# Raw weight buffers in turn, two tiles ahead, and a new memory layout in a fused attention and mixture-of-experts kernel

## The chip, the cores and the metric

The kernel runs on one core of a Trainium2 chip. Five engines run beside each other, each with its own queue of instructions: TensorE (PE; its weight loads are listed as PEld), VectorE (DVE), ScalarE (ACT), GpSimd (POOL) and SyncE (SP), which here only issues DMA transfers. The metric is the device time of one execution in microseconds, less is better.

## What is computed

Causal attention with a decay, for 8 batches of 8 heads, 576 positions of 64; its output, 4608 tokens of 512, goes through a mixture of 8 experts, of which each token takes the one with the highest logit:

```
scores = scale * q @ k.T + (cum[:, None] - cum[None, :])   # causal, cum = cumsum(log f)
x = softmax(scores) @ v                                    # 4608 tokens x 512
logits = x @ w_gate + modality_bias[modality_id]
e = argmax(logits); gate = softmax(logits)[e]
out = gate * (maximum(x @ w1[e], 0) @ w2[e])               # w1: 8 x 512 x 1024, w2: 8 x 1024 x 512
```

With the given inputs the experts 0 to 7 get 1053, 0, 0, 0, 90, 2200, 5 and 1260 tokens.

## The kernel before, in words

**Attention** (0 to about 365 us) runs over 32 pairs of heads. For each pair TensorE makes row maxima, the negative maxima are written to the tile `Sq` by two small shift DMAs on SP (`shift_out`, L638), the scores go to `ps`, ScalarE takes the exponential (L676, L682) and rounds it to `Ph` (L697), VectorE or GpSimd make the remainder `Pl` (L709), and TensorE multiplies with `v` into `po` or `pb` (L736 to L739). After each batch the routing chain on VectorE and GpSimd (`rm`, `rd`, `rc`, `rei`, `rtot`, ...) finds each token's expert and slot, and GpSimd scatters the rows to `xs` in device memory (`xs<-x`, L847), sorted by expert.

**The experts** work on tiles of tokens of one expert: 18 full tiles of 256 (`full(t)` for t = 0 to 17), then up to 8 half tiles of 128, of which 3 have tokens (`halves`, from about 783 us). For these inputs the full tiles belong to the experts 0, 0, 0, 5, 0, 5 (eight times, tiles 5 to 12), 7 (five times). A table in memory holds each tile's expert, its slot and a flag whether the expert differs from that of the tile before. Four tiles have their table from the counts after the next to last batch; the others get theirs in tile 2 (`other_tables`, some sixty small VectorE instructions on one row).

**Weights.** W1 and W2 of an expert have 2 MB each in float32. `load_w1` and `load_w2` fetch them by two DMAs of 1 MB each into a raw buffer; both carry the flag as a condition, and move nothing if the expert has not changed. Tile 1 has buffers of its own (`raw1b`, `raw2b`), all other tiles use `raw1` and `raw2`. The view of DMA names them `raw`. Because matmuls run in two-byte types, each weight is split into a scaled high half (float16, on ScalarE, L1303; from tile 2 on the last quarter on VectorE, L1301) and a low half (bfloat16, on VectorE, L1304): `w1h`, `w1l`, `w2h`, `w2l`, each with two buffers. The scale needs the largest magnitude: `scale` runs two passes of ScalarE over the raw weight (|w| summed up, L1255, "pass" in what follows; its output goes to the high half's buffer as scratch), adds over partitions by one small matmul on TensorE (L1257) and takes four small VectorE instructions (L1260 to L1263) to the power of two in `gs`.

**One tile.** `first` makes the hidden layer: 96 matmuls into three banks `ph` (L1379), in four groups of 24; ScalarE writes `hh` (L1393), VectorE `hl` (L1395), which free the bank. The fourth group takes the first group's bank. `second` makes the output: 48 matmuls into two banks `py` (L1428), ScalarE scales them to `y` (L1434), GpSimd writes the rows out (L1437). Tokens come as `xg`; VectorE turns them (`xt`, L1241), ScalarE and VectorE split them (`xh`, `xl`, L1356, L1357). While tile t multiplies, the passes, splits and tokens of tile t+1 are made.

**The order.** Each engine works through its instructions in order. A scheduler lists them by their dependencies and by lines such as `self.order(x, behind)` and `self.in_line(...)`, which put instructions one behind the other without a wait. SP issues its DMAs in that order too: one that waits holds up those behind it.

Of the kernel before, what the change touches and what calls it, by code (L numbers as in the profile page):

```python
# [224 lines left out]
class Attn:  # L225
    def __init__(self, ctx, tc, dram, qk, v, vt, f, ids, wg, bias, xs, writers, nb=8):
# [24 lines left out]
        self.divided, self.routed, self.weighed = [], {}, []  # L251
# [381 lines left out]
    def shift_out(self, p):  # L633

        self.own(("shift", p % 3), p)
        mT = self.get("mT", p)
        for a in range(2):
            x = self.nc.sync.dma_start(self.Sq[1 + a:P:64, p % 3, :], mT[:, a])  # L638
        self.shifted = x.ins.name
# [29 lines left out]
    def exp(self, p, g):  # L669
# [4 lines left out]
        if g == 2:  # L674

            nc.scalar.activation(ps[:, :, 0:w], ps[:, :, 0:w], AF.Exp, bias=self.lnp, scale=0.125)  # L676
            self.own(("Pt", p, g), p)
            return
# [13 lines left out]
    def half(self, p, i):  # L692
# [4 lines left out]
        x = self.nc.scalar.copy(self.Ph_t[p % 2][:, :, c], self.exps(p, i))  # L697
        self.rounded = x
# [4 lines left out]
    def rest(self, p, i):  # L703
# [5 lines left out]
        e.tensor_tensor(self.Pl_t[p % 2][:, :, c], self.exps(p, i), self.Ph_t[p % 2][:, :, c], ALU.subtract)  # L709
# [7 lines left out]
    def weighted(self, u):  # L717
# [22 lines left out]
        self.weighed = self.weighed[-1:] + [(first, x)]  # L740
# [263 lines left out]
class Moe:  # L1004
    def __init__(self, keep, tc, w1, w2, xs, writers, out):
# [7 lines left out]
        self.ring("xg", keep, 3, [P, 2 * 514], F32)  # L1013
        self.ring("xa", keep, 4, [P, T // P, 2], F32)
# [37 lines left out]
    def open(self, ctx):  # L1052
# [56 lines left out]
    def slots(self, nt, num, skip, name, rows=T):  # L1109
# [11 lines left out]
        e = t([1, 1 + num, 1], F32, "e")  # L1121
        vec.tensor_reduce(e[:, 1:], le, AX.X, ALU.add)
# [5 lines left out]
        if skip is not None:  # L1128
            vec.tensor_tensor(le, self.ie.broadcast_to(s3), e[:, 1:].broadcast_to(s3), ALU.is_equal)
# [10 lines left out]
    def table(self, e, k, cum, num, name, ok=None):  # L1140
# [4 lines left out]
        vec.tensor_copy(part(0), e[:, 1:])  # L1145
# [19 lines left out]
    def other_tables(self, n):  # L1165
# [20 lines left out]
        vec.tensor_copy(e[:, 0:1], self.last)  # L1186
        vec.tensor_reduce(eh[:, 0:1], e[:, 1:], AX.XY, ALU.max)

        vec.tensor_scalar(ok, ok, -1.0, 1.0, ALU.mult, ALU.add)
        vec.scalar_tensor_tensor(e[:, 1:], ok, eh[:, 1:2, :], e[:, 1:], ALU.mult, ALU.add)  # L1190
# [56 lines left out]
    def scale(self, name, t, raw, to, behind=None):  # L1247

        nc, vec = self.nc, self.nc.vector
        am, g, e, s = (self.next(x) for x in ("am", "gm", "ge", "gs"))  # L1250
# [497 lines left out]
```

## Time and profile before

| | |
|---|---|
| median of 3 runs | 826.67 us (826.48 to 828.06) |
| the profiled execution | 828.71 us, its span 827.0 |
| mean granted clock | 0.977 |
| busy TensorE / VectorE / ScalarE / GpSimd | 762.2 / 676.7 / 676.7 / 377.8 us |
| ScalarE idle ahead of the passes over W1 (L1255) | 17.6 us, behind loads of `raw` |

Times in the rows below are microseconds from the start of the span, unless marked ns. A row of a timeline is the start, the length, the engine, the line, the operation and its output and input by name, and in brackets the time for which the engine was idle before it, with the instruction that ended the wait. A row of waits is who waited, for whom, the total, how often and the longest. The chain is followed back from the last instruction; DMA in it is the time until a load landed. PEclk is TensorE's granted clock as a share of full speed.

### The profile page before, as it was taken

To read this page: it belongs to the slowest core of one execution; us is meant where nothing else is said; L and a number is where in the kernel's file an instruction comes from. 1 tells how busy PE (TensorE), PEld (TensorE's weight loads), DVE (VectorE), ACT (ScalarE), POOL (GpSimd) and SP (SyncE) were. 2 spreads that over 40 slices of the span, in tenths; PEclk is the share of its full clock that TensorE was granted. 3 is DMA by queue.
4 is the path that set the end of the run, shared out by engine and by line. 5 is a ranking of instruction groups with operands and counts; after the bars stand their busy time and mean duration, and the time that the engine had idled before them with its cause. 6 is when DMAs were issued, how large, how long until landed. Compare 5 with 4: busy or idle time off the path is not lost.

```text
span 827.0 us, 23639 instructions
## 1 busy us (share of the span) xinstructions
PE 762.2 (92%) x9567; PEld 563.7 (68%) x9567; DVE 676.7 (82%) x1393; ACT 676.7 (82%) x839; POOL 377.8 (46%) x374
## 2 busy tenths in 40 slices
PE   8998999989998999878788979999999989999996
PEld 4787887878887887674554556666666656666563
DVE  7887898989898989677548778888888788887777
ACT  5896989898989897688837488888888778888686
POOL 9766989898989887854240111111111010112011
PEclk9998999999999999999998999999999999999999
DMA  5533454545454433294983684212111451260931
GB/s 168 202 117 116 147 172 137 171 139 170 139 170 139 164 116 112 90 327 147 294 243 115 178 259 149 53 52 52 52 52 52 132 162 33 52 238 27 353 130 39
DMA packets 67583, 117.00 MB, mean 141 GB/s; under 512 B 10827, under 2 KB 27787, under 8 KB 67468
## 3 DMA queue, kind: packets, MB, share of 16 engines
q1 hardware_dynamic: 60746, 94.39, 36.1%
q0 software_dynamic: 6704, 21.02, 7.4%
q8 instruction: 77, 1.26, 0.7%
q14 instruction: 38, 0.31, 0.1%
q10 hardware_dynamic: 18, 0.01, 0.0%
HBM read 147.98 MB, written 22.55 MB: 206 GB/s over the span
## 4 chain that ended last, share of the span: by engine, by line
PE 50%; DVE 25%; ACT 7%; DMA 7%; issue 5%; POOL 5%; SPq 0%; DVEq 0%; ACTq 0%; POOLq 0%
PE py L1428 16%; PE ph L1379 15%; PE ps L592 7%; DMA raw<-in_w_dram 6%; DVE mt L613 4%; DVE vl L560 3%; PE po L736 2%; PE po L739 2%; POOL Pl L709 2%; PE po L738 2%; DVE w1l L1304 2%; PE pb L534 2%; DVE x L751 2%; POOL L L435 2%; PE ph L1495 1%
## 5 line engine op out<-in xcount | busy, mean ns | idle before, releaser
L1437 POOL DMA_INDIRECT out_dram<-y,xa x32 | 45.1, 1410 | 308.3 <-ACT y L1434 248.7
L709 POOL TENSOR_TENSOR Pl<-Pt,Ph 128x1024 f16<-128x1024 f32 (+1 forms) x63 | 141.7, 2255 | 14.6 <-ACT Ph L697 13.6
L1379 PEld LDWEIGHTS <-w1h 128*128 128x128 f16 x1152 | 112.4, 99 | 34.3 <-ACT w1h L1303 10.2
L1428 PEld LDWEIGHTS <-hh 128*128 128x128 f16 x576 | 55.5, 99 | 82.6 <-ACT hh L1393 14.4
L736 PE MATMUL po<-vh,Ph 128*128 128x73 f16 x930 | 101.8, 200 | 3.6 <-DVE lgh L754 3.4
L592 PE MATMUL ps<-X 64*128 64x288 f32 (+5 forms) x768 | 103.4, 339 | 0.0
L739 PE MATMUL po<-vh,Pl 128*128 128x73 f16 x930 | 101.4, 199 | 0.9 <-DVE Pl L709 0.9
L738 PE MATMUL po<-vl,Ph 128*128 128x72 f16 x930 | 101.6, 197 | 0.0
L682 ACT ACTIVATE Pt<-ps,lnp 128x576 f32<-128x576 f32 (+1 forms) x96 | 81.5, 864 | 20.2 <-PE ps L592 20.1
L736 PEld LDWEIGHTS <-Ph 128*128 128x128 f16 x960 | 94.3, 99 | 4.8 <-DVE lgh L754 1.6
L738 PEld LDWEIGHTS <-Ph 128*128 128x128 f16 x960 | 95.3, 99 | 3.3 <-issue 3.1
L739 PEld LDWEIGHTS <-Pl 128*128 128x128 f16 x960 | 94.3, 98 | 1.1 <-DVE Pl L709 1.0
L435 POOL TENSOR_TENSOR L<-raw,X 128x1152 bf16<-128x1152 f32 x32 | 84.6, 2642 | 20.5 <-ACT X L429 16.3
L1379 PE MATMUL ph<-xh,w1h 128*128 128x256 f16 x576 | 82.1, 276 | 12.1 <-DVE hl L1395 6.5
L1379 PE MATMUL ph<-xl,w1h 128*128 128x256 bf16 x576 | 89.3, 275 | 0.0
L1304 DVE SCALAR_TENSOR_TENSOR w2l<-raw,gs,w2h 128x1024 bf16<-128x1024 f32 x68 | 84.0, 1281 | 4.5 <-ACT w2h L1303 3.9
L613 DVE TENSOR_REDUCE mt<-ps 128x2 f32<-128x128 f32 (+3 forms) x128 | 81.5, 682 | 6.9 <-PE ps L592 6.8
L1379 PE MATMUL ph<-xh,w1l 128*128 128x256 f16 x576 | 86.2, 274 | 0.0
L1428 PE MATMUL py<-w2h,hh 128*128 128x512 f16 x288 | 77.3, 384 | 9.2 <-ACT hh L1393 7.3
L1304 DVE SCALAR_TENSOR_TENSOR w1l<-raw,gs,w1h 128x1024 bf16<-128x1024 f32 x68 | 84.3, 1280 | 1.0 <-ACT w1h L1303 0.4
L1428 PE MATMUL py<-w2l,hh 128*128 128x512 bf16 x288 | 78.8, 389 | 1.8 <-DVE w2l L1304 1.6
L1255 ACT ACTIVATE w1h<-raw 128x2048 f16<-128x2048 f32 x34 | 64.7, 1903 | 17.6 <-DMA raw<-in_w_dram 17.6
(340 smaller groups left out, 1912.0 us busy)
## 6 DMA issues: line engine op xcount, KB each, us to landing
raw<-in_w_dram SPq DMA_DIRECT2D x80, 1024.0 KB
raw<-in_qk_dram SPq DMA_DIRECT2D x32, 608.0 KB
vT<-in_vt_dram SPq DMA_DIRECT2D x32, 320.0 KB
xg<-xs SPq DMA_DIRECT2D x64, 128.0 KB
vr<-in_v_dram SPq DMA_DIRECT2D x30, 256.0 KB
raw1b<-in_w_dram SPq DMA_DIRECT2D x6, 1024.0 KB
raw2b<-in_w_dram SPq DMA_DIRECT2D x6, 1024.0 KB
hxg<-xs SPq DMA_DIRECT2D x5, 257.0 KB
```

Source lines behind the costliest of these rows:

```text
L435: e.tensor_tensor(self.two(self.L3[p % 3]), self.two(self.get("raw", p)), self.two(f32(X)), ALU.subtract)
L592: self.nc.tensor.matmul(ps[0:m, h, c:c + w], a(r), b(r), start=start, stop=not any(x[0] is ps for x in parts[n + 1:]), skip_group_check=True)
L613: nc.vector.tensor_reduce(mt[:, :, ic:ic + 1], pm[:, :, c0:c0 + w], AX.X, ALU.max)
L682: nc.scalar.activation(self.get("Pt", (p, i))[:, :, o:o + w], ps[:, :, 0:w], AF.Exp, bias=self.lnp, scale=0.125)
L709: e.tensor_tensor(self.Pl_t[p % 2][:, :, c], self.exps(p, i), self.Ph_t[p % 2][:, :, c], ALU.subtract)
L736: x = nc.tensor.matmul(o, Ph[:, c0:c0 + P], vh[:, c, hh, :], start=(c == 0), stop=False)
L738: nc.tensor.matmul(o[:, 1:73], Ph[:, c0:c0 + P], vl[:, c, hh, :], start=False, stop=False)
L739: x = nc.tensor.matmul(o, Pl[:, c0:c0 + P], vh[:, c, hh, :], start=False, stop=(c == ic))
L1255: made.append(nc.scalar.activation(to[a], raw[a], AF.Abs, accum_out=am[:, q:q + 1]))
L1304: return x, nc.vector.scalar_tensor_tensor(low, raw, s, high, ALU.mult, ALU.subtract)
L1379: y = nc.tensor.matmul(ph[g][:, i, :], w[:, k, f0:f0 + P], x[:, k, :], start=(j == 0 and (t > 0 or i == 0)), stop=(j == len(m) - 1 and (t ...
L1428: x = nc.tensor.matmul(py, h[:, k, c * P:c * P + P], w[:, k, :], start=(j == 0), stop=(j == len(m) - 1))
```

## The change

Each of W1 and W2 gets two raw buffers for all tiles, used in turn by t % 2. Tile t's loads fetch the weights of tile t+2, and the flag compares a tile's expert with that of two tiles before (`e` has two leading entries instead of one). Full tiles' loads then move data for the tiles 0, 1, 3, 6, 13 and 14; before, for 0 to 5 and 13. The first raw buffer of W1, `raw1a`, is taken from a pool that does not share memory with attention; its two DMAs and the first pass over it are placed inside attention's last pairs. The experts' memory is laid out in another order, the raw buffers low. The rules for the order of `hh` and the splits of W2 in tile 1 are gone, and in tile 0 the order of the passes is written out anew. Nothing is removed from the arithmetic.

```diff
@@ run
-        self.load_w1(self.row[0], 0, loads)
-        self.load_w2()
-        made, m, sc = self.scale("w1", 0, self.raw1[0], self.w1h[:, 0], self.routed["w0"].ins.name)
+        made = self.load_w1(self.row[0], 0)
+        self.in_line("so", *made, "sn")
+        for x in self.load_w2(0):
+            self.order(x, self.routed["sm"].ins.name)
+        self.load_w1(self.row[1], 1)
+        self.load_w2(1)
+        made, m, sc = self.scale("w1", 0)
...
-        self.in_line("Ph", *made, *[y[0] for y in x], a[0], *[y[0] for y in more[:2]], "odds", more[2][0])
+        self.in_line("h", made[0], "e")
+        self.in_line("Ph", made[1], *[y[0] for y in x], a[0], *[y[0] for y in more])
...
@@ full(t)
-            if t == 0:
-                self.load_w1(self.row[1], 1, always=True)
-                self.load_w2(1)
-                self.load_w1(self.row[2], always=True)
-            elif t > 1:
-                self.load_w1(self.row[t + 1])
+            if t + 2 > FULL:
+                self.load_w1(self.rowh[1], 1)
+            elif t and t != TABLES:
+                self.load_w1(self.row[t + 2], t % 2)
+            ec.setdefault(t, self.ec)
...
-                if t != 1:
-                    self.load_w2()
-                return made, names
+                if t != TABLES:
+                    self.load_w2(t % 2, ec[t])
+                return names
...
+                if t == 0:
+                    a, b = self.sums2
+                    self.in_line(more[-1][0], a, "odds", b, made[0], *self.later, made[1])
@@ first(t, again)
-            if g == 0:
-                rounded, behind = again(self.summed)
+            if t and g == int(t == OTHERS):
+                behind = again(self.summed)
...
-            if t == OTHERS:
-                self.order(x, behind[min(g + 1, 3)][0])
...
@@ open: the experts' memory
+        self.raw1a = keep.tile([P, 4, 1024], F32, name="raw1a")
-        raw1 = one([P, 4, 1024], F32, "raw1")
         self.w1h = one([P, 2, 4, 1024], F16, "w1h")
+        raw2 = one([P, 8, 512], F32, "raw2")
+        self.raw1 = self.raw1a, one([P, 4, 1024], F32, "raw1b")
+        self.raw2 = raw2, one([P, 8, 512], F32, "raw2b")
...
```

("h" and "e" are the round and the exponential of pair 30, "so" and "sn" the last shift DMA of pair 30 and the first of pair 31, "odds" ScalarE's `rex` of the routing.)

Three places show what that does to the order. SP at the end of attention, before (`raw_9435` is W1's buffer, `raw_9450` W2's):

```order
L638 DMA Sq<-mT 2x5x128 x4
L1199 TENSOR_LOAD c_taba x2
L1272 ISA
L1272 DMA raw_9435<-in_w_dram 128x4x512
L1272 ISA
L1272 DMA raw_9435<-in_w_dram 128x4x512
L1286 ISA
L1286 DMA raw_9450<-in_w_dram 128x4x512
```

and now (`raw1a` is W1's first buffer, `raw_9440` W2's):

```order
L638 DMA Sq<-mT 2x5x128 x2
L1196 TENSOR_LOAD c_taba x2
L1271 ISA
L1271 DMA raw1a<-in_w_dram 128x4x512
L1271 ISA
L1271 DMA raw1a<-in_w_dram 128x4x512
L638 DMA Sq<-mT 2x5x128 x2
L1284 ISA
L1284 DMA raw_9440<-in_w_dram 128x4x512
```

The load of the first W1 has moved ahead of the last two of the four shift DMAs; its table entries are read there too.

ScalarE around tile 0's hidden layer, before (`am` takes the sum of a pass, `gs` is a scale; `raw_9450` is W2, the second `xh` tile 1's tokens):

```order
L832 ACTIVATE rex<-rd,isw 128x40
L1303 ACTIVATE w1h<-raw_9435,gs_84 128x4x256
L1255 ACTIVATE w2h,am_69<-raw_9450 128x2048 x2
L1393 ACTIVATE hh<-ph_9417 128x512
L1393 ACTIVATE hh<-ph_9418 128x512
L1303 ACTIVATE w2h<-raw_9450,gs_85 128x1024 x4
L1393 ACTIVATE hh<-ph_9416 128x512
L1356 CAST xh_9458<-px_9412 128x4x128
L1356 CAST xh_9458<-px_9431 128x4x128
```

and now (`raw_9440` is W2 of tile 0, `raw1b` W1 of tile 1):

```order
L1302 ACTIVATE w1h<-raw1a,gs_85 128x4x256 x4
L1254 ACTIVATE w2h,am_70<-raw_9440 128x2048
L831 ACTIVATE rex<-rd,isw 128x40
L1254 ACTIVATE w2h,am_70<-raw_9440 128x2048
L1254 ACTIVATE w1h,am_71<-raw1b 128x4x512
L1302 ACTIVATE w2h<-raw_9440,gs_86 128x1024 x4
L1254 ACTIVATE w1h,am_71<-raw1b 128x4x512
L1355 CAST xh_9453<-px_9413 128x4x128
L1355 CAST xh_9453<-px_9432 128x4x128
L1393 ACTIVATE hh<-ph_9418 128x512
L1393 ACTIVATE hh<-ph_9419 128x512
```

The first two `hh` stood ahead of the splits of W2; they now stand behind them, behind both passes over tile 1's W1 and behind the two `xh`.

ScalarE between the last `hh` of tile 3 and the splits of W1 for tile 4, before (`raw_9435` is W1, `py_9426` and `py_9427` the two halves of tile 3's output, `xt` the turned tokens):

```order
L1393 ACTIVATE hh<-ph_9417 128x512
L1356 CAST xh_9457<-xt_9471 128x512
L1255 ACTIVATE w1h,am_68<-raw_9435 128x4x512
L1356 CAST xh_9457<-xt_9471 128x512
L1255 ACTIVATE w1h,am_68<-raw_9435 128x4x512
L1434 ACTIVATE y_9461<-py_9426,xs_91 128x512
L1434 ACTIVATE y_9462<-py_9427,xs_91 128x512
L1303 ACTIVATE w1h<-raw_9435,gs_86 128x4x256 x3
L1255 ACTIVATE w2h,am_69<-raw_9450 128x2048 x2
```

and now (`raw1a` and `raw_9440` hold W1 and W2 of tile 4):

```order
L1393 ACTIVATE hh<-ph_9418 128x512
L1254 ACTIVATE w1h,am_69<-raw1a 128x4x512 x2
L1254 ACTIVATE w2h,am_70<-raw_9440 128x2048
L1427 ACTIVATE y_9479<-py_9427,xs_92 128x512
L1427 ACTIVATE y_9480<-py_9428,xs_92 128x512
L1254 ACTIVATE w2h,am_70<-raw_9440 128x2048
L1302 ACTIVATE w1h<-raw1a,gs_87 128x4x256 x3
L1355 CAST xh_9452<-xt_9481 128x512 x2
```

The passes over W1 no longer stand between the two `xh`; a pass over W2 stands ahead of the two outputs and one behind them, and the `xh` have moved behind the splits of W1.

## Rows read from the trace of the kernel before

**Rows 1.** Stretches, tiles 1 to 4, 6: us, PE, PEld, DVE, ACT, POOL, PEclk, DMA, GB/s.
```profile
393.20:423.40 30.20, 23.57 (x147) 14.34 (x146) 19.60 (x28) 23.69 (x29) 11.98 (x17) 0.89 0.84 261
423.40:452.40 29.00, 22.52 (x148) 14.83 (x147) 16.84 (x40) 15.82 (x19) 2.94 (x3) 0.88 0.61 187
452.40:473.50 21.10, 21.07 (x146) 14.01 (x144) 18.21 (x65) 11.36 (x16) 2.22 (x2) 1.00 0.48 154
473.50:504.40 30.90, 23.47 (x148) 14.83 (x148) 22.76 (x35) 24.78 (x30) 2.08 (x2) 0.94 0.83 254
525.40:546.30 20.90, 20.90 (x148) 14.14 (x147) 18.56 (x28) 18.80 (x25) 3.45 (x2) 1.00 0.20 52
```

**Rows 2.** The chain that ended last, tile 6: start, us, what.
```profile
546.42 3.28 PE ph L1379 x30
556.92 1.73 PE py L1428 x8
```

**Rows 3.** TensorE's waits, 386 to 510: us in total, times, longest.
```profile
PE ph L1379 <- DVE hl L1395: 6.5, 1, 6.5
```

**Rows 4.** Waits of ScalarE in the same stretch.
```profile
ACT w1h L1255 <- DMA raw<-in_w_dram: 14.6, 5, 8.5
```

**Rows 5.** The chain that ended last, tiles 1 and 2.
```profile
397.83 13.89 DMA raw<-in_w_dram
414.87 2.07 DVE xt L1241 x2
416.94 4.84 DVE w1l L1304 x4
421.90 12.69 DMA raw<-in_w_dram
```

**Rows 6.** The chain that ended last, second layers of tiles 10 to 13.
```profile
621.32 8.65 PE py L1428 x40
665.68 10.49 PE py L1428 x40
688.41 8.65 PE py L1428 x40
```

**Rows 7.** TensorE's timeline: start, us, instruction; first layers of tiles 0 and 17.
```profile
367.04 0.61 PE L1379 MATMUL ph<-xh,w1h 128*128 128x256 f16 x4 [2.40 <-ACT w1h L1303]
...
760.87 0.61 PE L1379 MATMUL ph<-xh,w1h 128*128 128x256 f16 x4 [1.14 <-ACT w1h L1303]
```

**Rows 8.** SyncE's timeline at the end of attention (issues only).
```profile
338.80 8.10 SPq L638 DMA_DIRECT2D Sq<-mT  x4
348.67 1.35 SPq L1272 DMA_DIRECT2D raw<-in_w_dram  x2
```

**Rows 9.** ScalarE's timeline, last pair and tile 0.
```profile
350.07 1.09 ACT L676 ACTIVATE ps<-ps,lnp 128x1024 f32<-128x1024 f32 x1 [1.28 <-PE ps L592]
...
358.44 1.91 ACT L1255 ACTIVATE w1h<-raw 128x2048 f16<-128x2048 f32 x1
365.83 3.23 ACT L1303 ACTIVATE w1h<-raw,gs 128x1024 f16<-128x1024 f32 x3 [2.55 <-DVE z L749]
374.01 0.57 ACT L1393 ACTIVATE hh<-ph 128x512 f16<-128x512 f32 x1
375.94 4.27 ACT L1303 ACTIVATE w2h<-raw,gs 128x1024 f16<-128x1024 f32 x4
380.59 1.05 ACT L1356 CAST xh<-px 128x512 f16<-128x512 f32 x2
```

**Rows 10.** TensorE's timeline at the last pair's scores.
```profile
350.69 0.46 PE L592 MATMUL ps<-Sq,Sk 64*128 64x64 bf16 x12
```

**Rows 11.** Waits of the DMA queue on SyncE, 340 to 430.
```profile
SPq L1286 <- DMA xs<-x,rde: 19.3, 2, 16.9
```

**Rows 12.** VectorE's timeline, routing chain to the scale of W2.
```profile
367.35 0.20 DVE L779 TENSOR_REDUCE rm<-lg 128x5 f32<-128x40 f32 x1
...
375.70 0.15 DVE L1263 TENSOR_SCALAR gs<-ge 128x1 int32<-128x1 int32 x1
```

More of the change, by code (lines that the diff above doesn't have):

```diff
@@ L674, in exp @@
         if g == 2:
-            nc.scalar.activation(ps[:, :, 0:w], ps[:, :, 0:w], AF.Exp, bias=self.lnp, scale=0.125)
+            self.done["e", p] = nc.scalar.activation(ps[:, :, 0:w], ps[:, :, 0:w], AF.Exp, bias=self.lnp, scale=0.125)
             self.own(("Pt", p, g), p)
@@ L1245, in turn, with scale @@
         return [self.turned(self.xt[t], self.xg[t], k, k + 2) for k in (0, 2)]
-    def scale(self, name, t, raw, to, behind=None):
+    def scale(self, name, t, behind=None):
         nc, vec = self.nc, self.nc.vector
+        raw, to = (self.raw1, self.w1h) if name == "w1" else (self.raw2, self.w2h)
+        raw, to = raw[t % 2], to[:, t % 2]
         am, g, e, s = (self.next(x) for x in ("am", "gm", "ge", "gs"))
@@ L1265, in scale, with load_w1 @@
         return made, m, x
-    def load_w1(self, row, i=0, behind=None, always=False):
-        nc = self.nc
-        self.ec = self.val(row, 0, 7), None if always else self.val(row, 2, 1)
+    def load_w1(self, row, i):
+        nc, made = self.nc, []
+        self.ec = self.val(row, 0, 7), self.val(row, 2, 1)
         w1 = self.w1[bass.ds(self.ec[0], 1)].rearrange("o (p k) f -> p (o k) f", p=P)
         for q in range(2):
-            x = nc.sync.dma_start(self.raw1[i][:, :, q * 512:q * 512 + 512], w1[:, :, q * 512:q * 512 + 512], cond=self.ec[1])
-            if behind:
-                self.order(x, behind)
+            made.append(nc.sync.dma_start(self.raw1[i][:, :, q * 512:q * 512 + 512], w1[:, :, q * 512:q * 512 + 512], cond=self.ec[1]))
+        return made
     def order(self, x, behind):
@@ L1309, in split_w1 @@
             a = (slice(None), slice(None), slice(q * 256, q * 256 + 256))
[L1310 removed]
+            x, y = self.split(self.raw1[i][a], self.w1h[:, i][a], self.w1l[:, i][a], self.scales["w1", t][0], t > 1 and q == 3)
             behind = self.follow(behind, x, y)
@@ L1332, in split_w2 @@
             a = (slice(None), slice(2 * q, 2 * q + 2), slice(None))
-            x, y = self.split(self.raw2[t == 1][a], self.w2h[:, i][a], self.w2l[:, i][a], self.scales["w2", t][0], t > 1 and q == 3)
+            x, y = self.split(self.raw2[i][a], self.w2h[:, i][a], self.w2l[:, i][a], self.scales["w2", t][0], t > 1 and q == 3)
             for z in tabled:
@@ L1567, in early @@
         vec.tensor_tensor(left, io, base, ALU.subtract)
-        vec.scalar_tensor_tensor(k, e[:, 1:], float(CAP // T), left, ALU.mult, ALU.add)
-        ex = self.keep.tile([1, EARLY + 1, 1], F32, name="c_ex")
+        vec.scalar_tensor_tensor(k, e[:, 2:], float(CAP // T), left, ALU.mult, ALU.add)
+        ex = self.keep.tile([1, EARLY + 2, 1], F32, name="c_ex")
         vec.tensor_copy(ex, e)
@@ L1616, in again @@
             def again(begun):
-                made, *_ = self.scale("w2", t, self.raw2[t == 1], self.w2h[:, t % 2], begun)
+                made, *_ = self.scale("w2", t, begun)
+                self.sums2 = made
                 for x in made if t == 1 else ():
@@ L1640, in full @@
                 self.other_tables(n)
+                self.load_w1(self.row[t + 2], t % 2)
+                self.load_w2(t % 2)
                 self.load_x(t + 2)
```

98 lines of the change are left out of this document (44 added, 54 removed).

## The prediction, made before the changed kernel was run

> **What bounds the kernel now.** I read first the busy times by stretch, one stretch per full tile of the experts [rows 1]. TensorE's work for a tile is always the same: 96 matmuls of the first layer, 48 of the second, 147 or 148 instructions with the small ones. Where it never waits that takes 20.9 us [rows 1], 10.5 for the first layer (546.42 to 556.92 [rows 2]) and 10.4 for the second. Three tiles are far above: tile 1 with 30.2, tile 2 with 29.0, tile 4 with 30.9; in them TensorE is busy 22.5 to 23.6 us and its granted clock is 0.88 to 0.94. So 27.4 us lie in three places. TensorE's list of waits puts the longest down to VectorE's `hl`, 6.5 us [rows 3]; but ScalarE itself waited 14.6 us for loads of `raw` [rows 4], and the chain that ended last goes through two loads of 13.89 and 12.69 us [rows 5]: with one raw buffer per weight, the next tile's W1 is fetched only when this tile's has been split. Later there are two small losses: the change of expert before tile 13 (second layers at 621.32, 665.68 and 688.41: 44.36 and 22.73 us where 41.78 and 20.89 would do, so 2.6 and 1.8 lost [rows 6]), and 1.14 us in tile 17, whose first layer waits for W1's high half [rows 7]. Elsewhere the bound is TensorE, and the change takes no matmul away.
>
> **The sum's base.** All times are from the profiled execution (828.71 us, span 827.0). It is 2.0 above the median of 826.67; the difference worked out is taken from the median.
>
> **1. The start: W1 and its sums go into attention.** On SP the load of `raw1a` moves from behind the last two shift DMAs to ahead of them. They were issued by 346.9, the load at 348.67 [rows 8], 1.8 later; behind the pair of shifts before, near 339.9, it can go at 341.6. The same 2 MB had 9.8 us at most before (348.67 to their first pass at 358.44 [rows 9], to which ScalarE came no earlier); I take 8.4, so it is there at 350.0, at the latest at 351.4. What stands behind it on SP is the shift of pair 31, which TensorE's scores need from 350.7 [rows 10]. I take no delay; if it is late, all behind it is, by 0 to 3 us. The first pass itself, 1.90 us [rows 9], goes where ScalarE stood idle for 1.28 until 350.07 [rows 9]: the last pair is 0.6 late and 1.9 is saved behind it. `raw2`, `raw1b` and `raw2b` leave the memory for which W2's loads waited 19.3 us on scatters to `xs` [rows 11]; from 350 on, at 8.4 us for 2 MB, they are there by 358, 367 and 375, each before its first use. W1's scale is ready near 362.3 instead of 365.8, but attention's last products hold TensorE: first matmul at 365.3 instead of 367.04 [rows 7]. **Gain 1.7** (bounds 0 and 3.5).
>
> A rule speaks against this part. The Trainium skill, "DMA: Bandwidth & Descriptors", section "Queues, rings and completion order", says that SP owns one ring on each DMA engine and that a ring is consumed in order. By it the shift of pair 31 can't land before the 2 MB ahead of it have drained. No row of before shows such a pair of transfers; the need at 350.7 lies between 350.0 and 351.4, so the rule has its chance among the rivals.
>
> **2. Tile 0 loses.** ScalarE's new order has W1's four splits (4.3), two passes over W2 and one over tile 1's W1 (1.9 each), W2's four splits, a pass, two `xh`, and only then the four `hh`; before, two `hh` stood ahead of W2's splits [rows 9]. With the passes done at 372.4, ScalarE waits for W2's scale, which on VectorE stands behind the routing chain, from `rm` at 367.35 to `gs` at 375.70 [rows 12], 8.3 us; with `rm` a us earlier it comes at 374.5. Then 4.27 + 1.9 + 1.05 + 0.57: first `hh` at 382.3 instead of 374.6. TensorE has 72 of its 96 matmuls to do until about 374, waits some 8 us, and has 24 and 48 left, 13.0 us at full clock. I add 2 for a low clock on return and for W2's low halves on VectorE: the tile ends at 397.5 instead of 393.2. **Loss 4.3** (bounds: a gain of 1.7, if nothing waits; a loss of 8, if the clock stays low throughout).
>
> **3. Tile 1 loses less.** The scale of W1 now stands on VectorE behind W2's last low half, near 392.2. ScalarE from there: four splits (4.3), four passes with two outputs between (8.8), two `hh` (1.1), a pass (1.9), W2's four splits (4.3), two passes (3.8): 416.4. The sum's small matmul stands on TensorE with 40 of the second layer's 48 matmuls behind it: 8.6, and 1 for the clock. It ends at 426.0, before at 423.4: **2.6 behind**.
>
> **4. Tile 2 gains.** Its expert is tile 0's and still in its buffers: no load, 20.9 us instead of 29.0, end 446.9. Tile 3's weights are loaded a tile and a half ahead, hidden under 40 us of work. Some sixty small table instructions stand on VectorE ahead of the four low halves of its W2, as before; tile 3 took 21.1 us with them [rows 1] and takes 21.1 again: end 468.0, before 473.5: **5.5 ahead**. (If the table came late, the four low halves of 1.21 [rows 5] would hold up the second layer by 2 to 3.)
>
> **5. Tile 4 waits anew.** The small matmul of its W1's sum stands at the end of tile 3 (468.1); the scale takes 0.9. ScalarE does an output, a pass, three splits, two `xh`: 475. VectorE does a high split, a low split, two `xt` (2.07), three low splits, two `xl`, about 9 us [rows 5], with the first and the last two taken as 0.7 each: 478.0. Then 84 matmuls, 9.2 and 1.2 for the clock, and the second layer, 10.4 and 0.8 of waits: 499.6, before 504.4. **4.8 ahead**, though the tile takes 31.6 us and no load is left in it. Bounds: 15 ahead at 20.9 us, or level.
>
> **6. Steady tiles.** Passes for tile t+2 run in tile t. ScalarE was busy 18.80 and VectorE 18.56 of 20.9 [rows 1], and what they do stays. The pass over W2 uses W2's high half as scratch and so must wait for TensorE's last read. From there ScalarE has a pass, an output, a pass, an `hh` and three splits, 8.2 us; the next second layer begins after 10.5: hidden, 2 us to spare. The loads for tile 13 go out two tiles, some 40 us, ahead: **2.6 and 1.8 gained** (bounds 0 and 4.4). W1 of tile 17 is split ahead of the outputs: **1.1 gained**. The half tiles keep their order: 0, within 0.5. The new layout costs no instruction; its effect is on waits, counted in part 1.
>
> **Sum.** 4.8 + 2.6 + 1.8 + 1.1 = 10.3 us: 826.67 - 10.3 = **816.4**. Parts 2, 3 and 5 leave about 4 open: own range 812.5 to 820.5.
>
> **The rivals.** (a) *The front costs nothing.* If W2's scale is early in tile 0 and tile 4 waits less, 5 to 9 us more are won: 807.5 to 811.5, say 809.5. For it: all loads are there in time. Against it: ScalarE's order is fixed.
> (b) *The shift is late*, by the ring order: attention ends 1 to 3 us later, tiles 0 and 1 with it: 817.5 to 819.5, say 818.5.
> (c) *The front eats it all.* Waits in tiles 0, 1, 3 and 4 are each 2 to 2.5 longer, each with a stretch at the low clock behind it, 8 to 10 in all: 824.5 to 826.5 (823 to 828.3), about no change. That the change doesn't do what it says, a load that still waits for its buffer, falls in here. Beside it stands the Trainium skill, "Perfetto Trace Analysis", section "Identifying the Most-Contended Engine": kernels improve by way of their most-contended engine. That is TensorE, whose work is untouched; by that rule alone the time stays at 826.7. The trace agrees in the steady tiles only; tiles 1, 2 and 4 speak against it with 27.4 us.
> (d) *The ring of scratch and passes; slower.* If the pass over W2 waits for TensorE's last read longer than the 2 us to spare, every tile from 5 to 17 grows. From 10.3 / 13 = 0.79 us a tile on the kernel is slower than before; with a whole pass of 1.9 exposed it is 24.7 - 10.3 = 14.4 slower, 841. For it: ScalarE has 2.1 idle us in a tile and now a wait in its middle. Against it: the splits that the next second layer needs write the other buffer.
>
> **How the numbers follow.** Forecast 0.53, (a) 0.16, (b) 0.09, (c) 0.10, (d) 0.12. A measurement can tell about 0.2% (1.7 us) from no change. Faster than 825.0: the forecast, (a), (b) and a third of (c), 0.81. Within: the rest of (c), 0.07. Slower: (d), 0.12. The range leaves out (d) and the outer ends of (a) and (c): 807.5 to 825.5.
>
> **What would show it.** Right: no wait of ScalarE for a load between 386 and 510; TensorE idle some 8 us in tile 0 behind `hh`, and in tile 1 at the small matmul; tile 2 at 20.9; ahead of tile 4's first layer a wait of 8 to 10 us, ended by VectorE; no gap before tile 13. Wrong: steady tiles above 21 us, scores of the last pair that wait for the shift, or a tile 0 as short as before.

## The result and the profile after

The changed kernel takes 818.92 us in the median, the kernel before beside it 827.34: ratio 0.9898, 95% interval 0.9876 to 0.9919, so 8.4 us less (6.7 to 10.3). In a second series (`e0_after_again`) it was 814.97 beside 824.64, ratio 0.9889 (0.9862 to 0.9916). Predicted were 10.3 us less, 0.9875. The profiled execution took 820.75, its span 819.1 (before 828.71 and 827.0).

The stretches of the profile after, cut at its own tile borders: tiles 0 to 5, then tiles 11, 12 and 17 and the half tiles (columns as in [rows 1]):

```profile
367.00:401.80 34.80, 26.15 (x195) 17.36 (x196) 22.91 (x44) 23.35 (x28) 11.97 (x21) 0.90 0.34 114
401.80:430.90 29.10, 23.64 (x147) 14.65 (x147) 17.55 (x28) 26.38 (x32) 12.35 (x19) 0.88 0.83 272
430.90:451.80 20.90, 20.85 (x148) 14.15 (x147) 17.99 (x38) 13.98 (x18) 3.37 (x2) 1.00 0.05 16
451.80:472.50 20.70, 20.65 (x145) 13.94 (x144) 14.62 (x63) 12.43 (x15) 3.31 (x3) 1.00 0.30 77
472.50:502.00 29.50, 22.77 (x147) 14.81 (x147) 26.20 (x38) 27.63 (x33) 1.53 (x2) 0.88 0.56 179
502.00:523.10 21.10, 21.05 (x148) 14.29 (x148) 18.09 (x30) 19.45 (x24) 3.72 (x3) 1.00 0.17 51
...
627.50:648.40 20.90, 20.85 (x148) 14.14 (x147) 17.96 (x28) 18.27 (x23) 3.02 (x2) 1.00 0.80 252
648.40:669.30 20.90, 20.85 (x148) 14.12 (x147) 17.96 (x28) 18.26 (x23) 4.07 (x2) 1.00 0.80 252
...
752.90:773.80 20.90, 20.85 (x146) 14.25 (x146) 13.46 (x18) 10.64 (x13) 2.12 (x2) 1.00 0.90 318
773.80:819.00 45.20, 37.28 (x180) 22.03 (x182) 34.22 (x37) 34.12 (x44) 6.43 (x4) 0.98 0.30 98
```

Tile 2 fell from 29.0 to 20.9, and every later full tile but tile 4 is at the pitch of a tile that never waits. The loads for tile 13 now run in tile 11 and those for tile 14 in tile 12, at 252 GB/s each, and both tiles keep the 20.90 us: the loss of [rows 6] is gone, and so is the gap of [rows 7] ahead of tile 17. Tiles 1 and 4 stay long, and tile 0 is longer than before: three tiles, as before, though not the same three. TensorE's waits between 340 and 505 (us in total, times, longest) and two rows of its timeline say why:

```profile
PE py L1421 <- ACT hh L1393: 8.0, 3, 7.5
PE ph L1378 <- ACT xh L1355: 6.3, 1, 6.3
PE ps L1256 <- ACT w1h L1254: 3.8, 1, 3.8
PE ps L592 <- DMA Sq<-mT: 1.9, 1, 1.9
```

```profile
386.18 0.61 PE L1421 MATMUL py<-w2h,hh 128*128 128x512 f16 x1 [7.46 <-ACT hh L1393]
...
479.01 2.72 PE L1378 MATMUL ph<-xh,w1h 128*128 128x256 f16 x12 [6.33 <-ACT xh L1355]
```

The waits of [rows 3] and [rows 4] are gone: in the same stretch ScalarE's list of waits has no load in it. In their place stand waits for what ScalarE does first; why it comes late is tested below.

**Where to count from.** The two profiles do not reach the change at the same time. The shift DMAs of the last pair but one, where the change begins [rows 8], are issued at 340.80 in the profile after and at 338.80 before; in `e0_after_again`, the same program, at 336.20. The 40 us ahead of that point in these two profiles of one program (columns as in [rows 1]):

```profile
300.80:340.80 40.00, 35.57 (x616) 30.39 (x612) 33.98 (x88) 27.16 (x34) 28.45 (x24) 0.83 0.30 99
```

```profile
296.20:336.20 40.00, 36.52 (x732) 30.61 (x728) 35.93 (x103) 32.09 (x40) 33.12 (x32) 0.96 0.34 109
```

The granted clock is 0.83 in one and 0.96 in the other, in work that the change does not touch. So I count from that issue in every profile. All times in us; "rest" is the span after tile 5:

| profile | first matmul | tile 0 ends | tile 1 | tile 2 | tile 3 | tile 4 | tile 5 ends | rest |
|---|---|---|---|---|---|---|---|---|
| before | 28.2 | 54.4 | 30.3 | 29.0 | 21.0 | 31.0 | 186.7 | 301.5 |
| after | 28.3 | 61.0 | 29.1 | 20.9 | 20.9 | 29.5 | 182.3 | 296.0 |
| after again (e0) | 27.8 | 59.8 | 28.7 | 20.9 | 21.2 | 29.3 | 180.8 | 296.1 |
| e1, W1 behind | 28.7 | 62.1 | 29.6 | 20.9 | 20.9 | 29.8 | 184.1 | 296.1 |
| e2, half ahead | 26.5 | 60.3 | 29.6 | 20.9 | 20.9 | 29.8 | 182.3 | 295.9 |
| e3, tile 0's order | 27.5 | 53.0 | 29.9 | 20.9 | 22.3 | 30.3 | 177.3 | 296.1 |
| e4, tile 1's order | 26.8 | 60.2 | 25.9 | 21.1 | 21.1 | 29.6 | 178.8 | 295.5 |
| e5, tile 4's sum | 26.4 | 60.2 | 29.6 | 20.9 | 21.0 | 26.5 | 179.1 | 296.0 |
| e6, loads always | 26.3 | 59.2 | 29.2 | 20.9 | 20.9 | 35.6 | 186.6 | 297.8 |
| e7, old layout | 26.0 | 56.6 | 28.7 | 20.9 | 21.7 | 30.9 | 179.7 | 295.8 |
| e9, e3 + e4 + e5 | 27.1 | 52.6 | 25.9 | 25.5 | 26.2 | 23.4 | 174.4 | 295.8 |
| e10, e9 in old layout | 25.9 | 52.3 | 28.5 | 22.9 | 24.9 | 25.7 | 175.3 | 295.5 |

Up to tile 5 the two profiles after are 4.4 and 5.9 us ahead of before, behind it 5.5 and 5.4.

### The profile page after: what moved, and what is told of

Its sections match the earlier page's. It is cut to its first block, busy times and chain, and to the rows that moved or that the text cites. A ratio compares the mean times of both kernels' runs of the same rounds, so it can differ in the third digit from the quotient of the medians.

```text
span 819.1 us, 23695 instructions
## 1 busy us (share of the span) xinstructions
PE 760.8 (93%) x9545; PEld 566.1 (69%) x9567; DVE 679.4 (83%) x1392; ACT 676.7 (83%) x839; POOL 378.7 (46%) x374
## 4 chain that ended last, share of the span: by engine, by line
PE 55%; DVE 24%; POOL 8%; ACT 6%; issue 5%; DMA 1%; SPq 0%; ACTq 0%; DVEq 0%; POOLq 0%
PE py L1421 21%; PE ph L1378 19%; PE ps L592 5%; DVE mt L613 4%; DVE vl L560 4%; POOL Pl L708 4%; POOL L L435 3%; PE po L735 2%; DVE x L750 2%; DVE mt L618 1%; PE po L738 1%; DVE ps L615 1%; PE pb L534 1%; PE ph L1488 1%; PE po L737 1%
## 5 line engine op out<-in xcount | busy, mean ns | idle before, releaser
L1430 POOL DMA_INDIRECT out_dram<-y,xa x32 | 48.7, 1521 | 296.0 <-ACT y L1427 260.3
L592 PE MATMUL ps<-X 64*128 64x288 f32 (+5 forms) x768 | 104.3, 341 | 0.1
L1378 PE MATMUL ph<-xl,w1h 128*128 128x256 bf16 x576 | 86.6, 274 | 0.1
L1378 PE MATMUL ph<-xh,w1h 128*128 128x256 f16 x576 | 80.2, 276 | 6.6 <-ACT xh L1355 6.3
L1421 PE MATMUL py<-w2h,hh 128*128 128x512 f16 x288 | 75.5, 386 | 8.5 <-ACT hh L1393 8.0
L1421 PE MATMUL py<-w2l,hh 128*128 128x512 bf16 x270 | 74.0, 385 | 1.7 <-DVE w2l L1303 0.7
L697 ACT CAST Ph<-Pt 128x1152 f16<-128x1152 f32 (+1 forms) x64 | 69.7, 1098 | 2.0 <-PE po L738 0.5
L1421 PE MATMUL py<-w2h,hl 128*128 128x512 f16 x288 | 68.2, 379 | 0.0
L592 PEld LDWEIGHTS ps<-X 64*128 64x128 f32 (+1 forms) x768 | 62.0, 188 | 2.1 <-ACT X L429 0.4
```

The lines of the kernel that those rows point to most:

```text
L592: self.nc.tensor.matmul(ps[0:m, h, c:c + w], a(r), b(r), start=start, stop=not any(x[0] is ps for x in parts[n + 1:]), skip_group_check=True)
L697: self.done["h", p, i] = self.nc.scalar.copy(self.Ph_t[p % 2][:, :, c], self.exps(p, i))
L1378: y = nc.tensor.matmul(ph[g][:, i, :], w[:, k, f0:f0 + P], x[:, k, :], start=(j == 0 and (t > 0 or i == 0)), stop=(j == len(m) - 1 and (t ...
L1421: x = nc.tensor.matmul(py, h[:, k, c * P:c * P + P], w[:, k, :], start=(j == 0), stop=(j == len(m) - 1))
L1430: x = nc.gpsimd.indirect_dma_start(self.out, bass.IndirectOffsetOnAxis(ap=xa[:, c, 1:2].bitcast(I32), axis=0), y, None, bounds_check=NT - ...
```

## The experiments

Each diff is against the changed kernel. Each was timed beside the kernel before; its ratio is compared with 0.9889 (e0) and 0.9898.

### e0: the changed kernel again

> The changed kernel itself, once more, as the yardstick for the runs beside it. Expected: ratio to before 0.988 to 0.992. Its attention, on which the change acts only from 341 us on, shows how far a second profile lies from the first there: within 0.5 us of the kernel before if the 2.0 us by which the first profile of it was late at 341 were drift from run to run; again about 2 us late if the new memory layout or the longer program make attention itself slower.

Measured: 814.97 us, ratio 0.9889 (0.9862 to 0.9916); its attention is 2.6 us earlier than that of before, not 2.0 late, and not within 0.5 either. The lateness of the first profile was drift, which is larger than I expected, and single profiles must be counted from a point inside.

### e1 and e2: W1's load inside attention

```
-        self.in_line("so", *made, "sn")
+        self.in_line("sm", *made)
...
-        self.in_line("h", made[0], "e")
-        self.in_line("Ph", made[1], *[y[0] for y in x], a[0], *[y[0] for y in more])
+        self.in_line("Ph", *made, *[y[0] for y in x], a[0], *[y[0] for y in more])
```

> Undoes the placement inside attention alone: W1's load goes behind the last shift again and both passes of W1's sum stand behind the last scores, as in the kernel before; the new memory, the second buffers and all later orders stay. My theory (the placement wins 1.9 us of pass and loses the 1.9 us that the last scores waited for the shift behind the load): the wait of the scores on the shift is gone, the first matmul of tile 0 stays within 1 us of the changed kernel's, ratio to before 0.988 to 0.992, that is, the whole placement is worth nothing. Rival (the placement is a gain that run-to-run drift of attention hid): first matmul 2 to 4 us later, ratio 0.992 to 0.995. Second rival (the load costs more than the shift's 1.9 us, by traffic inside attention): faster than the changed kernel by over 1.5 us, ratio under 0.988.

Measured: 818.62 us, ratio 0.9921 (0.9895 to 0.9947). The time leans to 2 or 3 us slower; the intervals overlap, so it does not settle it alone. The profile is plainer. Both passes now stand behind the last pair on ScalarE:

```profile
355.22 1.91 ACT L1254 ACTIVATE w1h<-raw1a 128x2048 f16<-128x2048 f32 x1
...
357.12 1.89 ACT L1254 ACTIVATE w1h<-raw1a 128x2048 f16<-128x2048 f32 x1
```

The wait on the shift is gone, as expected, but in its place TensorE waits for the passes before it can finish the sum (e1's waits between 340 and 372; after and e0 have no such wait there):

```profile
PE ps L1256 <- ACT w1h L1254: 3.4, 1, 3.4
```

The scale of W1 is made 24.3 us after the shift's issue, against 23.0 to 23.8 in the five profiles whose start and tile 0 are the changed kernel's (after, e0, e4, e5, e6), and tile 0 ends at 62.1 against 59.2 to 61.0. The first matmul, at 28.7, is within 1 us of after's and e0's, as my theory said, but about 2 us behind that of e4, e5 and e6. So the profiles lean to a placement that is worth 1 to 3 us, against my theory that it is worth nothing; with one profile of e1, a mean clock of 0.83 in its second layer of tile 0 (e0 has 0.91), and times that overlap, that is not shown.

```
-        self.in_line("so", *made, "sn")
+        self.in_line("so", made[0], "sn")
+        self.in_line("sm", made[1])
```

> Only the first of the two 1 MB transfers of W1 is issued ahead of the last shift; the second behind it. Ring-order theory (a transfer of SP cannot land before what was issued ahead of it has drained, so half the bytes ahead is about half the delay): the scores of the last pair wait less than 0.5 us for the shift instead of 1.9, and the kernel is 1 to 2 us faster than the changed kernel, about 817.5 (ratio 0.9875). Rival (the shift is late for another reason, its source being written late or the traffic in general): the wait stays 1.5 to 2 us and the time stays within 0.5 us of the changed kernel.

Measured: 814.71 us, ratio 0.9885 (0.9856 to 0.9914): the changed kernel's own. In the changed kernel both 1 MB transfers go out ahead of the shift of pair 31, and its scores wait for it (first two rows, SyncE's and TensorE's timelines of after); in e2 one transfer goes ahead (last row), and no wait of `L592` on a DMA is left:

```profile
343.48 1.55 SPq L1271 DMA_DIRECT2D raw1a<-in_w_dram  x2
```

```profile
353.27 0.29 PE L592 MATMUL ps<-Sq,Sk 64*128 64x64 bf16 x4 [1.88 <-DMA Sq<-mT]
```

```profile
342.76 0.66 SPq L1271 DMA_DIRECT2D raw1a<-in_w_dram  x1
```

The wait was 1.88, 1.03, 0.85, 0.98 and 0.38 us in after, e0, e4, e5 and e6. So the mechanism of rival (b) is there, and the Trainium skill's rule that a ring is consumed in order ("DMA: Bandwidth & Descriptors", section "Queues, rings and completion order") agrees with these rows. The prediction made it too strict: in after the shift has landed at 353.13, while the last of the 16 parts of the second 1 MB lands at 354.76. The price of the wait does not show: e2 takes the same time, and its tile 0 ends at 60.3, as late as in the changed kernel, though its first matmul is 1.3 to 1.8 us earlier. What took that back is in step 2 of the account below.

### e3: tile 0's order on ScalarE

```
-   self.in_line(more[-1][0], a, "odds", b, made[0], *self.later, made[1])
+   h, w = self.hhs, self.later
+   self.in_line(more[-1][0], a, "odds", b, made[0], h[0], h[1], w[0], w[1], h[2], w[2], w[3], h[3], made[1])
```

> In tile 0 alone ScalarE's order is changed: two hidden outputs hh ahead of W2's splits, the third behind two splits and the last behind four, instead of all four behind pass, splits, pass and casts. Theory (tile 0 is long by ScalarE's order): TensorE's 7.5 us wait for hh falls under 2, the second layer of tile 0 ends about 393 to 395 instead of 401.8, tile 1 starts that much earlier; 6 to 8 us faster than the changed kernel, about 811 (ratio 0.981). Rival (what binds is W2's scale behind the routing chain on VectorE, and the splits then come as late): the wait for hh turns into a wait for W2's halves, and the gain is 0 to 3 us (816 to 819, ratio 0.987 to 0.990).

Measured: 811.1 us, ratio 0.9827 (0.9801 to 0.9853), 5 to 6 us less than the changed kernel, a little under the 6 to 8 expected. ScalarE's timeline in tile 0, of the changed kernel and of e3 (from the pass over tile 1's W1 on):

```profile
374.15 1.90 ACT L1254 ACTIVATE w1h<-raw1b 128x2048 f16<-128x2048 f32 x1
378.53 4.26 ACT L1302 ACTIVATE w2h<-raw,gs 128x1024 f16<-128x1024 f32 x4 [2.39 <-DVE gs L1262]
382.70 1.89 ACT L1254 ACTIVATE w1h<-raw1b 128x2048 f16<-128x2048 f32 x1
384.59 1.04 ACT L1355 CAST xh<-px 128x512 f16<-128x512 f32 x2
385.53 1.57 ACT L1393 ACTIVATE hh<-ph 128x512 f16<-128x512 f32 x3
```

```profile
370.13 1.90 ACT L1254 ACTIVATE w1h<-raw1b 128x2048 f16<-128x2048 f32 x1
372.02 1.06 ACT L1393 ACTIVATE hh<-ph 128x512 f16<-128x512 f32 x2
374.51 2.19 ACT L1302 ACTIVATE w2h<-raw,gs 128x1024 f16<-128x1024 f32 x2 [1.43 <-DVE gs L1262]
```

In the first, ScalarE idles 2.39 us for W2's scale with four `hh` behind it, on which TensorE waits 7.46; in the second two `hh` use that gap, and the longest wait for `hh` is 1.40. With the long wait the stretch of low clock is gone too: the granted clock is 1.00 from 365.1 to 390.6, all of e3's tile 0, against 0.90 in after's. Tile 0 ends 7.1 us earlier (53.0 against 60.1, the mean of after, e0, e4, e5 and e6). Of that 2.9 come back: tile 1 is 0.8 longer, tile 3 1.3 and tile 4 0.8 than where these are not edited. So the theory holds for the place, and in the profile 4.3 us are left behind tile 5 (177.3 against 181.6, the mean of after and e0).

### e4: tile 1's order on ScalarE

```
+                for x in made if t == 2 else ():
+                    self.order(x, self.relu)
+                self.relu1 = self.relu if t else None
...
+                if t == 2:
+                    for x in made:
+                        self.order(x, self.relu1)
```

> In tile 1 alone ScalarE's passes for later tiles (sums of tile 2's W2 and tile 3's W1) are put behind tile 1's four hidden outputs and W2's splits. Theory (tile 1 is 8 us long because passes that nobody waits for stand ahead of hh and the splits): tile 1 falls from 29.1 to 24 to 25.5 us and the kernel is 3.5 to 5 us faster than the changed kernel, about 814.5 (ratio 0.985). Rival (tile 1 waits for the scale of its W2, or for VectorE's low halves, so ScalarE's order does not matter): tile 1 stays above 28 us, the gain is under 1 us. A part may come back in tile 2 or 3, whose passes are now later: then tile 2 or 3 is above 21.5.

Measured: 812.21 us, ratio 0.9854 (0.9827 to 0.9881), some 3 us less; the interval overlaps the changed kernel's, and the profile is plainer. In the changed kernel W2's splits of tile 1 begin 9.6 us after the tile does (411.41 behind 401.79), in e4 6.8 (402.72 behind 395.88):

```profile
411.41 4.27 ACT L1302 ACTIVATE w2h<-raw2b,gs 128x1024 f16<-128x1024 f32 x4
```

```profile
402.72 4.27 ACT L1302 ACTIVATE w2h<-raw2b,gs 128x1024 f16<-128x1024 f32 x4 [0.88 <-DVE gs L1262]
```

Tile 1 takes 25.9 us, tiles 2 and 3 give back 0.2 each. The theory holds, a little under its low end: the splits now wait for W2's scale (0.88), of which the rival spoke.

### e5: tile 4's sum

```
             half, x, y = self.second(t)
+            if t == 3:
+                self.order(x, m.ins.name)
```

> In tile 3 alone TensorE's small matmul that finishes the sum of tile 4's W1 is moved ahead of half of tile 3's second layer. Theory (tile 4's first layer waits 6.3 us for xh, and 8.5 in all, only because that small matmul stands at the end of tile 3's second layer): the wait falls to 1 to 3 us, tile 4 from 29.5 to 23 to 25, the kernel 4.5 to 6 us faster than the changed kernel, about 813.5 (ratio 0.984). Rival (the passes over tile 4's W1 on ScalarE end only at 466.7 because its load, held until the table is stored, comes late): TensorE then waits for am in the middle of the second layer instead, and the gain is under 2 us.

Measured: 811.51 us, ratio 0.9838 (0.9812 to 0.9863), 4 to 5 us less. TensorE's small matmul and first matmul of tile 4 in e5; in after they stand at 472.51 and 479.01:

```profile
462.45 0.17 PE L1256 MATMUL ps<-am,conesb 128*128 128x2 bf16 x1
...
471.42 1.86 PE L1378 MATMUL ph<-xh,w1h 128*128 128x256 f16 x8 [3.60 <-ACT xh L1355]
```

The wait falls from 6.33 to 3.60 and tile 4 to 26.5, not to 23 to 25: between sum and first matmul lie 9.0 us of splits and casts now, 6.5 before, since ScalarE still has tile 3's passes and outputs to do. The place is right; in the profile the gain is half of what I expected.

### e6: every load made

```
-        self.ec = self.val(row, 0, 7), self.val(row, 2, 1)
+        self.ec = self.val(row, 0, 7), None
```

> Every full tile loads its W1 and W2 even when the expert is still in the buffer: about 4 MB per tile of 21 us. Two-tiles-ahead theory (a load that has two tiles of time is hidden, however many there are): steady tiles stay at 20.9 to 21.1, tile 2 too; only tile 4, whose load cannot be issued before the table is stored at about 461, grows, by 5 to 10 us; in all 824 to 829 (ratio 0.997 to 1.003). Rival (the loads are hidden only because most are left out; the memory traffic or the freeing of the buffers binds): steady tiles grow to 21.5 or more, 10 to 25 us in all, 834 to 850.

Measured: 822.37 us, ratio 0.9972 (0.995 to 0.9994). Tile 3, tile 4 and a steady tile:

```profile
445.50:466.40 20.90, 20.89 (x147) 13.98 (x144) 14.62 (x63) 10.99 (x13) 2.38 (x2) 1.00 0.60 218
466.40:502.00 35.60, 24.58 (x148) 15.88 (x149) 26.45 (x39) 29.75 (x37) 2.18 (x2) 0.81 0.99 301
```

```profile
543.70:564.60 20.90, 20.90 (x149) 14.12 (x147) 18.00 (x28) 18.35 (x23) 3.02 (x2) 1.00 0.80 253
```

At 253 GB/s instead of 52 a steady tile stays at 20.90: two tiles of lead hide the loads, whether they are left out or not. Tile 4, whose loads are issued late, takes 6 us more (35.6 against 29.3 to 29.6), at a clock of 0.81 and a DMA share of 0.99. Both as the theory says; that the work behind tile 5 would grow by 1.8 us, all of it in the half tiles, it did not say.

### e7 and e10: the memory in the old order

The diff restores the order of the pools of before, with the second raw buffers at the end; e10 has e3's, e4's and e5's edits as well.

> The memory of the experts laid out in the old order, with the second raw buffers appended; loads and orders are those of the changed kernel. Theory (the layout only lets the second W1 and W2 of the start load before the scatters of attention are done, and tile 1 does not wait for them at the end): loads of tile 0's W2 and tile 1's weights begin up to 20 us later, but the time is 0 to 1.5 us longer than the changed kernel's (ratio 0.989 to 0.992). Rival (the layout is what makes the front work): ScalarE waits 5 us or more for raw in tile 0 or 1 and the kernel is 4 to 10 us longer, 823 to 829.

Measured: 813.13 us, ratio 0.9869 (0.9838 to 0.99), no longer than the changed kernel; both theory and rival had it longer. W2's load of tile 0 goes out at 353.06 and tile 1's W1 at 361.20 (in e0 at 347.45 and 353.57, both attentions within 0.7 us), and ScalarE waits for no load but W1's first, 0.2 us. Tile 0 even ends 3.5 us earlier, but for another reason: in this layout the scheduler, which sets what no edit pins down, put all four `hh` of tile 0 ahead of the pass over tile 1's W1 and of W2's splits (the last `hh` at 375.09, that pass at 375.59), much as e3 does by hand. So e7 changes two things at once, and only e10 beside e9 tells what the layout alone is worth.

> The same three edits with the experts' memory in the old order, so that the loads of tile 0's W2 and of tile 1's weights wait for attention's scatters. With ScalarE's order of tile 0 written out, what is left between this and the kernel beside it is the earlier loading itself. Theory (the early 6 MB buy nothing, and their traffic delays TensorE in attention's last products by 1 to 2 us, as the gaps with no named releaser of 0.6 to 1.3 us there say, which the old layout and the late load did not show): first matmul 1 to 2 us earlier counted from the last shifts, the whole 0 to 2 us faster than the kernel beside it. Rival (tile 1's weights come too late once tile 0 is short): ScalarE waits for raw in tile 0 or 1, 2 to 6 us slower than the kernel beside it.

Measured: 809.61 us, ratio 0.9801 (0.9763 to 0.9838), and e9 beside it 0.9799 (0.9764 to 0.9833): the same. The first matmul is 1.2 us earlier, as the theory says, and tile 1 is 2.7 longer, as the rival says: ScalarE's passes over tile 1's W2 wait for its load (timeline of e10).

```profile
393.38 1.91 ACT L1254 ACTIVATE w2h<-raw2b 128x2048 f16<-128x2048 f32 x1 [1.61 <-DMA raw2b<-in_w_dram]
396.53 1.91 ACT L1254 ACTIVATE w2h<-raw2b 128x2048 f16<-128x2048 f32 x1 [1.15 <-DMA raw2b<-in_w_dram]
```

Neither reaches the end: at the end of tile 0 0.3 us of the earlier start are left, tiles 2 and 3 are 3.9 us shorter than e9's and tile 4 2.4 longer, and behind tile 5 e10 is 0.9 us later. With tile 0's order written out, the new layout is worth nothing that these times can measure; with the changed kernel's own order it was not tested.

### e9: the three orders together

> The three order edits in one kernel: tile 0's hidden outputs ahead of W2's splits, tile 1's later passes behind its own work, tile 4's small matmul ahead of half of tile 3's second layer. One by one the profiles put them, counted from the same point in attention to the end of tile 5, at 4.3, 2.8 and 2.5 us ahead of the changed kernel. Theory (three places, three causes, so the gains add): 8 to 10 us faster than the changed kernel, ratio to before 0.977 to 0.980, about 806. Rival (the waits share VectorE, and what one place wins the next gives back, as tile 0's 7.3 us did: 3 of them came back in tiles 1, 3 and 4): 4 to 6 us, ratio 0.982 to 0.984, no better than tile 0's edit alone.

Measured: 808.94 us, ratio 0.9799: 7 to 8 us faster than the changed kernel, the best of all. By its ratio it is at the edge of the theory, by the profile between theory and rival: the parts add up to 9.6 us (4.3, 2.8 and 2.5 at the end of tile 5) and the profile shows 7.2. Its tiles 1 to 4 together take 100.9 us, spread nearly evenly (the rows below), where after has 100.4 in two peaks. So the 7 us lie in tile 0, and what the other two edits do is to keep them (e3 alone has 103.4 in these tiles). TensorE's longest waits there are for ScalarE's passes over W1 (5.3 us in two) and for VectorE's `hl` (2.9 in one); no run tests these:

```profile
388.90:414.70 25.80, 22.80 (x147) 14.53 (x147) 14.14 (x26) 24.44 (x30) 9.67 (x18) 0.93 0.73 232
414.70:440.20 25.50, 22.59 (x148) 14.83 (x147) 22.32 (x46) 16.92 (x21) 5.14 (x4) 0.93 0.28 97
440.20:466.40 26.20, 22.85 (x146) 14.40 (x145) 21.20 (x69) 17.47 (x20) 3.86 (x3) 0.93 0.28 73
466.40:489.80 23.40, 21.21 (x147) 14.23 (x148) 20.16 (x30) 22.49 (x28) 1.47 (x1) 1.00 0.70 212
```

## Why the prediction held, step by step

The predicted 10.3 us less and the measured 8.4 (6.7 to 10.3) agree in mechanism and nearly in size; counted inside the profiles it is 9.9 and 11.3. That the sum comes out is in part luck: its errors in tiles 0 and 4 cancel.

1. **The start.** Gain 1.7 predicted. The first matmul comes at 26.3 to 28.3 instead of 28.2: a gain of 0 to 2, 1.1 in the mean of the five profiles whose tile 0 is the changed kernel's (after, e0, e4, e5, e6). Two things that I had at nothing take the rest: the shift waits behind the load (0.4 to 1.9), and TensorE stands still for its own instructions (last section). In e2, which has neither, the first matmul comes at 26.5, where I had it.
2. **Tile 0.** Predicted to end 4.3 later than before; 4.8 to 6.6 measured. Where it stands was right to the instruction: `hh` behind the pass, the splits and the casts, a wait of 7.46 where I had some 8. Two terms were mis-sized. In after and e0 it is the start: the first matmul is 1.8 and 1.3 later than the 26.5 that I had, and all behind it is late. In e2, e4 and e5 the start is as predicted, W2's scale and the second layer come 1.0 to 1.7 earlier than in after and e0, and still the tile ends within 0.2 of their mean (60.4): there it is the clock. While TensorE waits for `hh`, its granted clock falls to 0.50, the lower of its two levels, for 6.8 us in after and e0 and for 10.2 in e2, e4 and e5. First the second layer up to the tile's end, then the low stretch inside it and ahead of it, each of e0 and of e2 (columns as in [rows 1]):

```profile
381.04:396.01 14.97, 14.80 (x76) 7.61 (x77) 13.92 (x18) 7.61 (x10) 0.00 (x0) 0.91 0.24 60
377.00:383.70 6.70, 2.67 (x9) 1.27 (x10) 2.69 (x4) 4.95 (x8) 2.77 (x5) 0.50 0.40 140
```

```profile
383.89:400.35 16.46, 16.29 (x76) 8.37 (x77) 13.93 (x18) 7.62 (x10) 0.00 (x0) 0.83 0.22 55
379.50:389.60 10.10, 5.71 (x23) 3.40 (x24) 4.27 (x5) 5.31 (x8) 3.00 (x5) 0.50 0.49 145
```

   Length times clock is 13.5 to 13.7 us in after, e0, e2, e4, e5 and e6: the same work. So my 13.0 and 2 for it were about right for after and e0 (15.6 and 15.0) and over 1 us short for e2, e4 and e5 (16.3 to 16.5). In e6 the low stretch is as long but begins earlier in the wait, and the tile ends at 59.2. Why it is longer in some profiles than in others is not shown. (The prediction's sum is also 0.2 off: 382.3, 13.0 and 2 make 397.3.)
3. **Tile 1.** 28.5 us predicted, 28.7 to 29.6 measured; its end was to be 2.6 behind, and is 3.8 and 5.4 behind in e0 and after, the error of tile 0 carried on.
4. **Tiles 2 and 3.** 20.9 and 21.1 predicted, 20.9 and 20.9 to 21.2 measured; all 8 us of tile 2 came.
5. **Tile 4.** 31.6 predicted, 29.3 to 29.8 measured. VectorE's work ends where I had it, 9.9 us behind the sum (472.51 and 482.40). But the 84 matmuls that I put behind it begin 0.8 earlier, when the first of the two `xl` is done; they take 9.4 us, not 10.4, since the low clock ends at 482.3, and the second layer takes 10.9, not 11.2. And the wait that was to be 8 to 10 us, ended by VectorE, is 6.33, ended by ScalarE's `xh`: the first twelve matmuls (479.01) need only `xh` and W1's high half.

```profile
477.54 3.65 DVE L1303 SCALAR_TENSOR_TENSOR w1l<-raw1a,gs,w1h 128x1024 bf16<-128x1024 f32 x3
481.10 1.30 DVE L1356 TENSOR_TENSOR xl<-xt,xh 128x512 bf16<-128x512 f32 x2
481.85 1.25 PE L1378 MATMUL ph<-xl,w1h 128*128 128x256 bf16 x8
```

   So at the end of tile 4 the kernel is 4.3 and 5.7 us ahead (4.8 predicted): the errors of tiles 0 and 4 cancel, which nothing in the prediction foresaw.
6. **Steady tiles and the end.** 5.5 predicted (2.6, 1.8 and 1.1), 5.4 and 5.5 measured; the half tiles are 0.4 longer, within the 0.5.

The rivals: (a) was shut out by ScalarE's order, as said against it, though e9 shows that another order gives 809. (b) came true as a wait; its 817.5 to 819.5 holds the measured 818.9 as well as the forecast's own range does, and what speaks against it as the account is e2, which takes the same time without the wait. (c) did not come: the kernel got 1% faster with TensorE's work untouched, and e9 2%, because TensorE's waits got shorter; the prediction's reading, that the time can change only with the work of the most-contended engine, was too narrow. (d) did not come: the steady tiles take 20.9 us each.

What stays open: how much the placement of W1's load is worth, since the timed intervals of e1 overlap the changed kernel's, and why the low clock in tile 0 lasts 6.8 us in some profiles and 10.2 in others.

## What to carry to other kernels

Hiding a load only moves the bound to the next engine in the row: here each weight must be summed, scaled and split on ScalarE and VectorE, and in three tiles an order of instructions, ScalarE's in tiles 0 and 1 and TensorE's own ahead of tile 4, took back or kept a large part of what the hidden loads could have given. When loads or buffers change, look at what then stands first on the engine behind them: work for a later tile can stand ahead of work that the busiest engine waits for now, and one change of order (e3) gave back 4 to 6 us. Follow a gain at the start of a stage to the stage's end, and look at the granted clock on the way: in tile 0 the start's gain of 1.0 to 1.7 us reached the second layer and was lost there to a longer stretch of low clock.

## What the runs showed of the hardware

TensorE stands still twice in attention's last products while nothing that the profile shows holds it (releaser "issue"), in the profile after:

```profile
360.69 0.21 PE L738 MATMUL po<-vh,Pl 128*128 128x73 f16 x1 [1.34 <-issue]
...
367.46 0.19 PE L735 MATMUL pb<-vh,Ph 128*128 128x73 f16 x1 [1.05 <-issue]
```

Both gaps are there in after, e0, e3 and e9 (1.2 to 1.3 and 0.6 to 1.1 us), one of 0.6 and 0.8 in e4 and e5, none in before, e1, e2, e6, e7 and e10. Where both are, the first matmul comes at 27.1 to 28.3; with one or none, under the early load, at 25.9 to 26.8.

The DMA packets in the traces tell what TensorE waits for. After's page lists a queue of instructions (packets, MB, share of 16 engines):

```profile
q8 instruction: 77, 1.26, 0.6%
```

Its packets have 16 KB, and from one to the next TensorE starts 252 to 256 matmuls and weight loads (the median of each profile). The gaps lie ahead of the same two instructions in every profile that has them, 255 apart, and each ends 2.2 to 2.5 us after a packet of q8 has begun (in after at 358.42 and 365.06). Where there is no first gap, that packet begins 3.0 to 4.9 us before TensorE comes to the instruction. So TensorE stands still for its next block of instructions, which comes late: with the first gap the packet begins 4.0 to 4.7 us after the instruction 255 places ahead of it, without it 0.5 to 2.9. The Trainium skill, "Runtime: NRT & Kernel Launch", section "Instruction fetch mechanics", says that each engine's sequencer fetches its instructions in blocks through a DMA queue of its own; the 16 KB packets of q8 agree. The late packets fall into the time when 8 MB of weights are fetched at a DMA share of about 1, but e1, e2 and e6 have that traffic without a gap, so what makes the packets late is not shown.

The other surprise is how far profiles of one program lie apart before they reach the change: the same shift is issued at 336.20 and 340.80, at granted clocks of 0.96 and 0.83 ahead of it.
